# Emission order kept on every engine, a multiply-and-accumulate for the denominators, and first-tile silus in groups of two

## The chip, the cores and the metric

The kernel runs on one core of one Trainium2 chip. The metric is the device time of one execution in microseconds. Three timed runs of the kernel before gave 1099.16 us as the median, from 1097.7 to 1101.51. Names of engines are those of the profile: PE is the matmul engine, PEld its loads of weights, DVE the vector engine, ACT the activation engine, POOL the general engine, SP the engine that issues most DMAs. A line number such as L505 is a line of the kernel before; the kernel after is shorter by two to three lines there, and rows of its order carry its own numbers.

## The reference

Attention with random features over 8 batches of 8 heads, 576 tokens and 64 dimensions, followed by one layer of a perceptron with silu over the 4608 tokens. All of it is float32; the weights of the perceptron come as 64-bit floats.

```python
def phi(x):
    proj = np.einsum('bhsd,md->bhsm', x, omega)
    sq = np.sum(x * x, axis=-1, keepdims=True) / 2.0
    h = proj - sq
    h = h - np.max(h, axis=-1, keepdims=True)
    return np.exp(h) / np.sqrt(m)
q_p, k_p = (phi(q_s), phi(k_s))
kv = np.einsum('bhsm,bhsd->bhmd', k_p, v)
z = np.sum(k_p, axis=2)
num = np.einsum('bhsm,bhmd->bhsd', q_p, kv)
den = np.einsum('bhsm,bhm->bhs', q_p, z)[..., None] + 1e-06
attn = num / den
...
h = x @ w_in
g = h * (1.0 / (1.0 + np.exp(-h)))
out = g @ w_out
```

## The kernel before

**Attention.** It goes by pairs of heads, 32 of them (n = 0 to 31), each a `hk` and a `hq` of nine chunks of 128 tokens by 128 features. The middle chunk holds the last 64 tokens of one head and the first 64 of the other. For a pair, SP loads the raw keys and queries, the same in natural order (`nat`), and the values. ACT squares `nat` (L250) and DVE sums it (`sqk`, `sqq`, L254). PE projects (L262, and the middle chunk at L269), DVE takes the maxima (`mxk`, `mxq`, L276 and L278) and makes the shift `nbk`, `nbq` in two instructions (L282, L283). ACT does the exp: for the first eight pairs chunk by chunk from PSUM (L298), for the others DVE first lowers the values into SBUF (L303, L306) and one exp follows (L312). POOL adds the keys' chunks up to `es` (L318, L320, L323), PE sums `es` over the tokens and spreads the sum to all partitions (L327), ACT copies it to `zb` (L335, L336), three versions of 128 columns: one head, middle, other head. PE makes the product of keys and values (L343), ACT copies it (`kt`, L348), PE turns it (L351), ACT copies it again (`kw`, L356).

**Denominators.** DVE multiplies `hq` by `zb` in three instructions (chunks 0 to 3, 4, 5 to 8; L362) into `prod`, which has a 129th column of guard values in each chunk, set once by POOL (L219). DVE then sums `prod` over 129 columns into `den`, nine values per partition (L369), and takes the reciprocal `rd` (L370). POOL multiplies `hq` by `rd` in three groups of chunks (L375), PE transposes them (L381), ACT copies them to `en` (L385), and PE makes the numerator (L399), which is the attention's result: ACT writes its high part `xh` (L413), DVE the rest `xl` (L418).

**Weights.** There are 32 chunks of 512 KB, sixteen of each matrix. Each is loaded by SP (`wraw`, L435), and turned from 64-bit floats to 32-bit ones by ACT (`wre`, L442) and three DVE instructions (L456, L458, L462), then split by POOL into a high and a low part (L476, L480). The parts of the second matrix go out to HBM (L483) and are loaded again for each step (L487).

**Perceptron.** Nine tiles of 512 tokens: four pairs fill a tile, and the ninth holds the 64 tokens left over from each batch. A tile has 16 steps f of 128 hidden features, 144 steps in all. A step is stage one (L495, twelve matmuls into a bank `ps_h`), silu on ACT twice (`gh`, rounded, L500; and in place in PSUM, L501), `gl` on DVE, which is their difference and frees the bank (L505), and stage two (L513, twelve matmuls into four banks `ps_acc`).

**What sets the order.** The class `Plan` lists units of work with an engine, a duration, a key (when it is due) and what they need, simulates them, and picks for each engine the ready unit with the least key; a change of ACT's function adds 8 to the key and 1.3 to the duration. PSUM has two banks `h`, two `att` and four `acc`; attention may borrow from `h` and `acc` early on, by the key of the unit. The units are emitted in the order that `plan.run()` returns. The layer below, the tile framework, then places the emitted instructions on each engine, and moves instructions past one another as it sees fit where data allow it. Loads of tables for ACT's functions are added by the compiler where exp and silu alternate.

Of the kernel before, what the change touches and what calls it, by code (L numbers as in the profile page):

```python
# [8 lines left out]
F32 = mybir.dt.float32  # L9
# [4 lines left out]
ALU = mybir.AluOpType  # L14
# [4 lines left out]
P = 128  # L19
# [44 lines left out]
class Plan:  # L64
# [16 lines left out]
    def run(self):  # L81
# [29 lines left out]
        def bank_pools(u):  # L111
            pools = ["att"]
            if u["key"] < clock(LAG) - 1:
                pools.append("acc")
            if u["key"] < START_MLP - 1:
                pools.append("h")
            chosen, when, used = [], 0.0, {p: 0 for p in pools}
            for _ in range(u["banks"]):
                best = None
                for p in pools:  # L120
                    t = slot_time(p, used[p])
                    if t is not None and (best is None or t < best[0]):
                        best = (t, p)
                if best is None:
                    return None, None
                used[best[1]] += 1
                chosen.append(best[1])
                when = max(when, best[0])
            return chosen, when
# [68 lines left out]
def attention_mlp(ctx: ExitStack, tc: tile.TileContext, qT, kT, qn, kn, v, om_in, w_in, w_out, out):  # L198
# [16 lines left out]
    nc.vector.memset(ones, 1.0)  # L215
    omr = const.tile([P, M], F32, tag="omr", name="omr")
    oms = const.tile([P, M], F32, tag="oms", name="oms")
    prod = const.tile([P, NC, M + 1], F32, tag="prod", name="prod")
    nc.gpsimd.memset(prod, GUARD)  # L219

    def bank(pool):
        return pools[pool].tile([P, 512], F32, tag=pool, name=f"ps_{pool}")
# [132 lines left out]
        T["kw", n] = kw = new("kw", [P, P])  # L355
        nc.scalar.copy(kw, T.pop(("kwp", n))[:, :P])  # L356

    def products(n):
        e, zb = T["h", n, "q"], T.pop(("zb", n))
        for j, (lo, hi) in enumerate(((0, 4), (4, 5), (5, 9))):  # L360
            c = slice(lo, hi)
            nc.vector.tensor_tensor(  # L362
                prod[:, c, :M], e[:, c], zb[:, j].unsqueeze(1).broadcast_to([P, hi - lo, M]), ALU.mult
            )

    def denom(n):
        den = new("den", [P, NC])
        T["rd", n] = rd = new("rd", [P, NC])
        nc.vector.tensor_reduce(den, prod, AX.X, ALU.add)  # L369
        nc.vector.reciprocal(rd, den)  # L370

    def normal(n, g):
# [175 lines left out]
    for n in range(NWIN):  # L548
# [67 lines left out]
        if not merged:  # L616
# [5 lines left out]
            free=[("kt", n)])  # L622
        add(("kw", n), "ACT", 0.3, at(n, 6.8, 36.7), lambda n=n: kw_copy(n), after=[("ktt", n)], order=[("kw", n - 1)] if n else [],
            alloc=[("kw", ("kw", n))], free=[bk(("ktt", n))])
        add(("prod", n), "DVE", 1.7, at(n, 8, 34.2), lambda n=n: products(n),
            after=e["q"] + [("zc", n)], order=[("den", n - 1)] if n else [], free=[("zb", n)])
        add(("den", n), "DVE", 1.6, at(n, 8.1, 34.4), lambda n=n: denom(n), after=[("prod", n)],
            alloc=[("den", ("den", n)), ("rd", ("rd", n))])
        plan.freed_by[("den", n)] = [("den", n)]
        for g in range(3):  # L630
            add(("norm", n, g), "POOL", 0.85, at(n, 9 + 0.1 * g, 37 + 0.1 * g), lambda n=n, g=g: normal(n, g),
# [57 lines left out]
    for i, (t, f) in enumerate(steps):  # L689
        key = clock(i)  # L690
        late = i >= total - LAG
        add(("get", t, f), "SP", 0.42, clock(i + LAG - AHEAD_OUT), lambda t=t, f=f: get_weight(t, f),
            after=[("keep", f)], order=[("get",) + divmod(i - 1, NF)] if i else [],
            alloc=[("wo", ("wo", t, f))], lat=2.1)
        for k in range(NK):
            x = [("restin", k)] if t == B else [("xl", NPAIR * t + k, 0)]
            w = [("wlo", "in", f)] if t == 0 else []
            add(("s1", t, f, k), "PE", 0.69, key + 0.945 * k, lambda t=t, f=f, k=k: stage1(t, f, k),
                after=x + w, order=[done] if done else [], alloc=[] if k else [("h", ("ph", t, f))],
                free=[("x", t, k)] if f == NF - 1 else [])  # L700
            done = ("s1", t, f, k)
        add(("silu", t, f), "ACT", 1.22, key + STEP * 0.55, lambda t=t, f=f: silu(t, f), after=[("s1", t, f, NK - 1)],
            alloc=[("gh", ("gh", t, f))], table="silu")
        add(("gl", t, f), "DVE", 0.7, key + STEP * 0.7, lambda t=t, f=f: g_low(t, f), after=[("silu", t, f)],
            alloc=[("gl", ("gl", t, f))], free=[("ph", t, f)])
        for j in range(4):
            k2 = clock(i + LAG + 0.5) + 0.945 * j
            if late:
                k2 = clock(total) + 4 + 4 * j + i - total
            alloc = [("acc", ("po", t, x)) for x in range(4)] if f == 0 and j == 0 else []  # L710
            w = [("get", t, f)]
            prior = [("s2",) + divmod(i - 1, NF) + (3 if not late else j,)] if i and (late or not j) else []
            if j:
                prior.append(("s2", t, f, j - 1))
            add(("s2", t, f, j), "PE", 0.69, k2, lambda t=t, f=f, j=j: stage2(t, f, j),
                after=[("gl", t, f)] + w, order=prior, alloc=alloc,
                free=[("gh", t, f), ("gl", t, f), ("wo", t, f)] if j == 3 else [])
            if f == NF - 1:
                add(("store", t, j), "ACT", 0.62, k2 + 0.2, lambda t=t, j=j: store(t, j), after=[("s2", t, f, j)],
                    free=[("po", t, j)])  # L720
    for u in plan.run():
        u["fn"](*[bank(p) for p in u["pools"]])


_OUT = ((B * S, DMODEL), "float32")
# [48 lines left out]
```

## Time and profile before

| what | value |
|---|---|
| runs, median (lowest, highest) | 1099.16 us (1097.7, 1101.51) |
| the profiled execution | 1101.4 us |
| its span | 1099.3 us, so 2.1 us outside |
| mean granted clock of PE | 0.976 |
| PE busy | 1053.1 us, 96% of the span |
| DVE, ACT, POOL busy | 566.4, 583.1, 255.5 us |
| table loads of ACT at L312, L500 | 48 and 56, 1283 ns each |

The page gives, by line, what an engine did and what it waited for. Busy shares over the whole span say little here: the start has little PE work and the rest is full of it, so the stages are read one by one. `gl` (L505) comes once in a step, and its starts are the milestones by which steps are counted in what follows: the first is at 100.00 us, the second at 107.70, the seventeenth, which ends the first tile's sixteen, at 225.10.

### The profile page before, as it was taken

Reading aid. Unit: us, or ns where it says so; the run is one execution under the profiler, and the core shown is the slowest. Engines: PE = TensorE matmul, PEld = TensorE weight load, DVE = VectorE, ACT = ScalarE, POOL = GpSimd, SP = SyncE. Lnnn points to the kernel's source line nnn. Section 1 sums busy time; section 2 is a strip of 40 time slices with the busy share of each in tenths; the row PEclk is TensorE's granted clock in tenths of the full one; section 3 lists DMA queues with packets and bytes.
Section 4 is the critical chain, followed back from the end, with each engine's and each line's share of the span. In section 5 each row is a group of like instructions: output and inputs, shape, how many; then the busy total and the mean of one; then the engine's idle time right before and its main releaser. Section 6 shows DMA issues by size and latency. Waiting matters only on the chain.

```text
span 1099.3 us, 16192 instructions
## 1 busy us (share of the span) xinstructions
PE 1053.1 (96%) x5900; PEld 834.5 (76%) x5900; DVE 566.4 (52%) x1109; ACT 583.1 (53%) x1085; POOL 255.5 (23%) x327
## 2 busy tenths in 40 slices
PE   5677998899999999999999999999999999999998
PEld 4455776687877778777778777787877788888886
DVE  6788897745555455545555455555554431111111
ACT  5557878565556555555556555655565442222211
POOL 3666665411111111111111111111111110000000
PEclk7688999999999999999999999999999999999999
DMA  7576787553335443444345433533343226223323
GB/s 282 198 221 234 265 290 252 182 167 125 124 126 178 139 133 119 136 165 138 122 139 178 140 127 130 173 131 126 123 154 104 80 80 213 96 96 122 109 96 96
DMA packets 66526, 167.84 MB, mean 153 GB/s; under 512 B 15632, under 2 KB 15760, under 8 KB 66448
## 3 DMA queue, kind: packets, MB, share of 16 engines
q1 hardware_dynamic: 65984, 166.23, 45.6%
q8 instruction: 47, 0.77, 0.3%
q10 hardware_dynamic: 464, 0.59, 0.1%
q14 instruction: 31, 0.25, 0.1%
HBM read 146.87 MB, written 19.92 MB: 152 GB/s over the span
## 4 chain that ended last, share of the span: by engine, by line
PE 86%; DVE 5%; DMA 3%; ACT 3%; POOL 1%; issue 1%; SPq 0%; ACTq 0%; DVEq 0%; POOLq 0%
PE ps_acc L513 35%; PE ps_h L495 34%; PE ps_att L262 5%; PE ps_att L343 3%; PE ps_att L381 3%; PE ps_att L399 2%; DMA wraw<-w_out 1%; DMA nat<-qn 1%; PE ps_att L327 1%; PE ps_att L269 1%; DVE w L458 1%; ACT hq L298 1%; DVE w L462 1%; POOL hq L375 1%; DVE den L369 1%
## 5 line engine op out<-in xcount | busy, mean ns | idle before, releaser
L513 PE MATMUL ps_acc<-wo,gh 128*128 128x512 f32 x1152 | 369.9, 402 | 0.0
L500 ACT ACTIVATE gh<-ps_h 128x512 fp32r<-128x512 f32 x144 | 86.2, 599 | 295.9 <-PE ps_h L495 295.3
L505 DVE TENSOR_TENSOR gl<-ps_h,gh 128x512 fp32r<-128x512 f32 x144 | 99.1, 688 | 275.8 <-ACT ps_h L501 275.8
L513 PEld LDWEIGHTS ps_acc<-wo,gh 128*128 128x128 f32 x1152 | 207.1, 189 | 43.7
L495 PE MATMUL ps_h<-xh,wh 128*128 128x512 f32 x576 | 235.0, 409 | 0.3 <-ACT xh L413 0.3
L495 PE MATMUL ps_h<-xh,wl 128*128 128x512 f32 x576 | 226.7, 394 | 0.0
L495 PE MATMUL ps_h<-xl,wh 128*128 128x512 f32 x576 | 225.9, 392 | 0.0
L513 PE MATMUL ps_acc<-wo,gl 128*128 128x512 f32 x576 | 225.8, 392 | 0.0
L375 POOL TENSOR_TENSOR hq<-hq,rd 128x384 f32<-128x384 f32 x96 | 81.7, 879 | 421.4 <-DVE rd L370 396.5
L495 PEld LDWEIGHTS ps_h<-xh,wh 128*128 128x128 f32 x576 | 108.1, 188 | 24.7 <-issue 0.8
L513 PEld LDWEIGHTS ps_acc<-wo,gl 128*128 128x128 f32 x576 | 108.1, 188 | 24.2 <-issue 0.8
L495 PEld LDWEIGHTS ps_h<-xh,wl 128*128 128x128 f32 x576 | 108.1, 188 | 24.1
L495 PEld LDWEIGHTS ps_h<-xl,wh 128*128 128x128 f32 x576 | 108.5, 188 | 22.3 <-DVE xl L418 0.4
L312 ACT ACT_TABLE_LOAD x48 | 61.6, 1283 | 69.2 <-DVE hq L303 53.3
L318 POOL TENSOR_TENSOR t<-hk 128x256 f32<-128x256 f32 x64 | 48.8, 780 | 183.2 <-ACT hk L312 170.1
L278 DVE TENSOR_REDUCE mxq<-ps_att 128x4 f32<-128x512 f32 x57 | 37.2, 687 | 99.7 <-PE ps_att L262 99.6
L501 ACT ACTIVATE ps_h<-ps_h 128x512 f32<-128x512 f32 x144 | 85.3, 593 | 0.0
L500 ACT ACT_TABLE_LOAD x56 | 71.8, 1283 | 22.0 <-PE ps_h L495 21.3
L362 DVE TENSOR_TENSOR prod<-hq,zb 128x512 f32<-128x512 f32 (+1 forms) x96 | 52.3, 595 | 49.6 <-ACT zb L336 47.7
L250 ACT ACTIVATE nat<-nat 128x576 f32<-128x576 f32 x64 | 44.6, 703 | 20.3 <-DMA nat<-kn 12.3
L381 PE MATMUL ps_att<-ident,hq 128*128 128x128 f32 x261 | 41.1, 284 | 7.9 <-POOL wp L476 2.4
L278 DVE TENSOR_REDUCE mxk<-ps_att 128x4 f32<-128x512 f32 x55 | 35.6, 686 | 18.7 <-PE ps_att L262 18.7
(121 smaller groups left out, 1232.0 us busy)
## 6 DMA issues: line engine op xcount, KB each, us to landing
wo<-wo_d SPq DMA_DIRECT2D x144, 512.0 KB, 3.3
rawk<-kT SPq DMA_DIRECT2D x32, 352.0 KB, 3.0
rawq<-qT SPq DMA_DIRECT2D x32, 352.0 KB, 3.8
v<-v SPq DMA_DIRECT2D x32, 320.0 KB, 2.9
nat<-kn SPq DMA_DIRECT2D x32, 288.0 KB, 3.3
nat<-qn SPq DMA_DIRECT2D x32, 288.0 KB, 3.2
wraw<-w_in SPq DMA_DIRECT2D x16, 512.0 KB, 4.6
wraw<-w_out SPq DMA_DIRECT2D x16, 512.0 KB, 4.3
```

What stands on the lines that cost most here:

```text
L262: nc.tensor.matmul(ps[:, i * M : (i + 1) * M], raw[r, o : o + P], oms[r], start=True, stop=True)
L278: nc.vector.tensor_reduce(m[:, 5 * j : 5 * j + 4], ps.rearrange("p (c m) -> p c m", m=M), AX.X, ALU.max)
L312: nc.scalar.activation(h, h, AF.Exp)
L318: nc.gpsimd.tensor_tensor(t[:, j], e[:, 5 * j : 5 * j + 2], e[:, 5 * j + 2 : 5 * j + 4], ALU.add)
L362: nc.vector.tensor_tensor(prod[:, c, :M], e[:, c], zb[:, j].unsqueeze(1).broadcast_to([P, hi - lo, M]), ALU.mult)
L375: nc.gpsimd.tensor_tensor(e[:, c], e[:, c], rd[:, c].unsqueeze(2).broadcast_to([P, 3, M]), ALU.mult)
L381: nc.tensor.transpose(ps[:, i * P : (i + 1) * P], T["h", n, "q"][:, 3 * g + i], ident)
L495: nc.tensor.matmul(ph, w[:, k, :], x, start=k == 0 and n == 0, stop=k == NK - 1 and n == 2)
L500: nc.scalar.activation(gh, ph, AF.Silu)
L501: nc.scalar.activation(ph, ph, AF.Silu)
L505: nc.vector.tensor_tensor(gl, T["ph", t, f], T["gh", t, f].bitcast(F32), ALU.subtract)
L513: nc.tensor.matmul(T["po", t][j], g[:, js], w, start=f == 0 and n == 0, stop=f == NF - 1 and n == 2)
```

## The change

There are four edits.

1. The loop that emits the units stands in `tc.manual_schedule()`: the framework keeps the emitted order on every engine.
2. The three products and the sum of a pair's denominators become nine `tensor_tensor_reduce`, one per chunk, each multiplying `hq` by `zb`, adding up over the 128 columns from the start value GUARD, and giving one column of `den`. On DVE each is two instructions, the second of which reads the accumulator. `prod` loses its guard column and the memset on POOL. In the plan one unit `den` of 2.3 us takes the place of `prod` (1.7) and `den` (1.6).
3. In the first tile (t = 0) the silu of an even step waits for stage one of the odd step behind it, and its key is later by one step, so that two silus stand together.
4. Attention may no longer borrow banks `h` once the first stage one is placed.

```diff
-            if u["key"] < START_MLP - 1:
+            if u["key"] < START_MLP - 1 and ("s1", 0, 0, 0) not in end:
                 pools.append("h")
...
-    prod = const.tile([P, NC, M + 1], F32, tag="prod", name="prod")
-    nc.gpsimd.memset(prod, GUARD)
+    prod = const.tile([P, NC, M], F32, tag="prod", name="prod")
...
-    def products(n):
+    def denom(n):
         e, zb = T["h", n, "q"], T.pop(("zb", n))
-        for j, (lo, hi) in enumerate(((0, 4), (4, 5), (5, 9))):
-            c = slice(lo, hi)
-            nc.vector.tensor_tensor(
-                prod[:, c, :M], e[:, c], zb[:, j].unsqueeze(1).broadcast_to([P, hi - lo, M]), ALU.mult
+        den = new("den", [P, NC])
+        for c in range(NC):
+            j = (c >= MID) + (c > MID)
+            nc.vector.tensor_tensor_reduce(
+                out=prod[:, c], in0=e[:, c], in1=zb[:, j], scale=1.0, scalar=GUARD, op0=ALU.mult, op1=ALU.add,
+                accum_out=den[:, c : c + 1],
             )
-
-    def denom(n):
-        den = new("den", [P, NC])
         T["rd", n] = rd = new("rd", [P, NC])
-        nc.vector.tensor_reduce(den, prod, AX.X, ALU.add)
         nc.vector.reciprocal(rd, den)
...
-        add(("prod", n), "DVE", 1.7, at(n, 8, 34.2), lambda n=n: products(n),
-            after=e["q"] + [("zc", n)], order=[("den", n - 1)] if n else [], free=[("zb", n)])
-        add(("den", n), "DVE", 1.6, at(n, 8.1, 34.4), lambda n=n: denom(n), after=[("prod", n)],
-            alloc=[("den", ("den", n)), ("rd", ("rd", n))])
+        add(("den", n), "DVE", 2.3, at(n, 8, 34.2), lambda n=n: denom(n), after=e["q"] + [("zc", n)],
+            order=[("den", n - 1)] if n else [], alloc=[("den", ("den", n)), ("rd", ("rd", n))], free=[("zb", n)])
...
-        add(("silu", t, f), "ACT", 1.22, key + STEP * 0.55, lambda t=t, f=f: silu(t, f), after=[("s1", t, f, NK - 1)],
+        pair = t == 0 and f % 2 == 0
+        add(("silu", t, f), "ACT", 1.22, key + STEP * (1.55 if pair else 0.55), lambda t=t, f=f: silu(t, f),
+            after=[("s1", t, f + pair, NK - 1)],
             alloc=[("gh", ("gh", t, f))], table="silu")
...
-    for u in plan.run():
-        u["fn"](*[bank(p) for p in u["pools"]])
+    with tc.manual_schedule():
+        for u in plan.run():
+            u["fn"](*[bank(p) for p in u["pools"]])
```

How instructions stand on the engines, at three places. PE in the startup, between the transposes of pair 0 (`ident,hq`) and the projections of pair 2 (`oms,rawk`); `es,ones` is the sum over tokens of pair 1, `hk,v` its product of keys and values, `en,kw` the numerator of pair 0. Before:

```order
L381 MATMUL ps_att<-ident,hq 128x128 x6
L327 MATMUL ps_h<-es,ones 128x256
L343 MATMUL ps_att<-hk,v 64x128 x10
L399 MATMUL ps_acc<-en,kw 64x512 x2
L399 MATMUL ps_att<-en,kw 64x64 x2
L262 MATMUL ps_acc<-oms,rawk 128x128 x8
```

After:

```order
L378 MATMUL ps_att<-ident,hq 128x128 x6
L342 MATMUL ps_att<-hk,v 64x128 x10
L396 MATMUL ps_acc<-en,kw 64x512 x2
L396 MATMUL ps_att<-en,kw 64x64 x2
L326 MATMUL ps_acc<-es,ones 128x256
L350 MATMUL ps_acc<-ident,kt 128x128
```

The sum over tokens stood ahead of the other two and now stands behind them.

DVE at the denominators of pair 2; `sqq` is the sum of squares for the queries of pair 3, `mxk` maxima of the keys of later pairs. Before:

```order
L362 TENSOR_TENSOR prod<-hq,zb 128x4x128
L362 TENSOR_TENSOR prod<-hq,zb 128x128
L362 TENSOR_TENSOR prod<-hq,zb 128x4x128
L254 TENSOR_REDUCE sqq<-nat 128x9
L369 TENSOR_REDUCE den<-prod 128x9
L278 TENSOR_REDUCE mxk<-ps_att 128x4
L370 RECIPROCAL rd<-den 128x9
```

After, from the last of the nine chunks on:

```order
L362 ISA prod,den<-hq,zb 128x128
L362 ISA den 128x1
L367 RECIPROCAL rd<-den 128x9
L253 TENSOR_REDUCE sqq<-nat 128x9
L277 TENSOR_REDUCE mxk<-ps_att 128x4 x2
```

The sum of squares stood between the products and their sum, and now stands behind the reciprocal; nothing stands between the chunks.

ACT in the first tile, at the exps of the keys of pair 7 and the silus around them. Before:

```order
L298 ACTIVATE hk<-ps_att,nbk 128x128 x8
L385 COPY en<-ps_att 128x384
L500 ACT_TABLE_LOAD
L500 ACTIVATE gh<-ps_h 128x512
L385 COPY en<-ps_att 128x384
L298 ACT_TABLE_LOAD
L298 ACTIVATE hk<-ps_att,nbk 128x128
L501 ACT_TABLE_LOAD
L501 ACTIVATE ps_h<-ps_h 128x512
```

After:

```order
L297 ACTIVATE hk<-ps_att,nbk 128x128 x8
L382 COPY en<-ps_att 128x384
L497 ACT_TABLE_LOAD
L497 ACTIVATE gh<-ps_h 128x512
L498 ACTIVATE ps_h<-ps_h 128x512
L497 ACTIVATE gh<-ps_h 128x512
L498 ACTIVATE ps_h<-ps_h 128x512
L382 COPY en<-ps_att 128x384
L297 ACT_TABLE_LOAD
L297 ACTIVATE hk<-ps_att,nbk 128x128
```

One step's two activations stood on both sides of an exp with a table load ahead of each; now the four activations of two steps stand behind one load. Over the whole program the order has 120 table loads before and 108 after; up to the seventeenth `gh` there are 28 and 16.

## The prediction

> **What bounds the kernel now.** I read the table of stages first, then single starts of `gl`, then the chain of waits up to 225 us, then the timelines of DVE and ACT. The profiled execution took 1101.4 us, of which the span is 1099.3; 2.1 us lie outside it. The columns of the table are the stretch, its length, each engine's busy time with its count of instructions, TensorE's granted clock and the DMA share.
>
> ```profile
> core 0: us, PE busy (x) PEld busy (x) DVE busy (x) ACT busy (x) POOL busy (x), PEclk, DMA share, GB/s
> 0.00:107.70 107.70, 74.47 (x459) 52.77 (x460) 83.18 (x152) 66.83 (x191) 63.80 (x76) 0.76 0.70 233
> 107.70:225.10 117.40, 109.13 (x599) 82.97 (x598) 94.95 (x161) 89.22 (x169) 65.95 (x67) 1.00 0.71 242
> 250.00:850.00 600.00, 599.79 (x3546) 478.76 (x3545) 325.03 (x678) 340.02 (x572) 113.94 (x166) 1.00 0.42 138
> ```
>
> From 250 us on PE is never idle and runs at the full clock: every other engine has room, and only fewer matmuls could shorten that stretch. The change removes none. The idle PE time lies ahead: 33.2 us of it (107.7 − 74.47) before the second `gl`, at 107.70, and 8.3 us (117.4 − 109.13) in the first tile, up to the 17th, at 225.10. The next rows are the second and the seventeenth `gl`, and `gl` alone counted in the two last stretches.
>
> ```profile
> 107.70 0.69 DVE L505 TENSOR_TENSOR gl<-ps_h,gh 128x512 fp32r<-128x512 f32 x1
> 225.10 0.69 DVE L505 TENSOR_TENSOR gl<-ps_h,gh 128x512 fp32r<-128x512 f32 x1 [3.21 <-ACT ps_h L501]
> 107.70:225.10 117.40, 10.14 (x15) 1.00 0.71 242
> 250.00:850.00 600.00, 56.52 (x82) 1.00 0.42 138
> ```
>
> Fifteen steps take 117.4 us in the first tile, 7.83 each; later 82 take 600 us, 7.32 each. At the later pace the fifteen are 109.8 us. So the first tile has 7.6 us to give by its steps and 8.3 by PE's idle time, which agree. Everything behind 225.10, 874 us of the span, I take as unchanged: the order on PE there is the same in both kernels, and PE is full.
>
> In the startup DVE has 83.18 busy of 107.70 us, more than any other engine. Two places of it show what the order costs. On PE, for pair 1:
>
> ```profile
> 27.25 0.90 PE L381 MATMUL ps_att<-ident,hq 128*128 128x128 f32 x3 [0.33 <-POOL hq L375]
> 33.65 1.22 PE L327 MATMUL ps_h<-es,ones 128*128 128x256 f32 x2 [5.50 <-POOL es L323]
> 36.99 1.84 PE L399 MATMUL ps_acc<-en,kw 128*64 128x512 f32 x4
> ```
>
> PE stands 5.50 us for POOL's `es` of pair 1, with the k-v product of pair 1 and the numerator of pair 0 queued behind; pair 0's transposes ended at 28.15. And on DVE, for pairs 1 and 2:
>
> ```profile
> 40.87 0.88 DVE L362 TENSOR_TENSOR prod<-hq,zb 128x128 f32<-128x128 f32 x2
> 42.33 1.35 DVE L369 TENSOR_REDUCE den<-prod 128x9 f32<-128x1161 f32 x1
> 44.20 0.21 DVE L370 RECIPROCAL rd<-den 128x9 f32<-128x9 f32 x1
> 55.83 1.59 DVE L362 TENSOR_TENSOR prod<-hq,zb 128x512 f32<-128x512 f32 x3
> 58.83 0.76 DVE L254 TENSOR_REDUCE sqq<-nat 128x9 f32<-128x576 f32 x1 [1.41 <-ACT nat L250]
> 59.50 1.35 DVE L369 TENSOR_REDUCE den<-prod 128x9 f32<-128x1161 f32 x1
> 61.37 0.20 DVE L370 RECIPROCAL rd<-den 128x9 f32<-128x9 f32 x1
> ```
>
> Pair 2's products end at 57.42, yet `den` starts at 59.50, since a sum of squares whose square came late stands between. The chain shows what it waited for, and two durations:
>
> ```profile
> 19.25 1.49 DVE prod L362 x3
> 53.83 4.20 DMA nat<-qn
> 59.58 1.27 DVE den L369
> ```
>
> **The change, part by part. Order kept.** It moves rows on all five engines and adds no work. For pair 1 the k-v product and the numerator go ahead of the wait for `es`. They may start at about 28.5 rather than at 34.8 and 36.99. DVE then has the low part of pair 0 done before pair 1's `zb` (its sum ends at 34.87, four copies of ACT follow, about 36). The denominators of pair 1 may start near 36.2; with 2.4 us for them (below) and 0.12 for the reciprocal, `rd` is ready near 39 where it was at 44.20: 5 us. For pair 2 `den` no longer stands behind the late sum of squares: that is another 3 us at 61.37 (from 57.42, and 2.4 us of work that starts at 55.83, against 61.37), but the next pair's shift needs that same sum, and the load of `qn` (4.20 us) that it waits for isn't shortened, so I count pair 2's as partly hidden. What is late next is DVE's own work: 83.18 of 107.70 us. Bounds for the startup: 0, if other waits (the loads of `qn`, POOL's norms) take the place; 10, if both gains and some of the 24.5 idle DVE us go. I take 5, the gain of pair 1 alone, handed on whole.
>
> Against it, an order that is fixed can put DVE, ACT or SP behind a head that waits. Where a dependent pair stands together on DVE it costs little: the rows below show 0.20 from the start of the first to the start of the second (228.58 to 228.78) and 0.07 where a stranger follows (76.86 to 76.93), so 0.13 each. There are 20 more such pairs of shifts in the whole program and 32 of `den` and reciprocal; nine of 32 pairs of heads lie before 225.10, so at most (20 + 9) × 0.13, about 4 us of DVE, which the 24.5 idle us cover in part. I leave it in the lower half of the range.
>
> ```profile
> 228.58 0.17 DVE L282 TENSOR_TENSOR nbk<-mxk,sqk 128x8 f32<-128x8 f32 x1
> 228.78 0.17 DVE L283 SCALAR_TENSOR_TENSOR nbk<-nbk,sqk 128x8 f32<-128x8 f32 x1
> 97.29 0.28 DVE L276 TENSOR_REDUCE mxk<-ps_att 128x1 f32<-128x128 f32 x1
> 97.49 0.20 DVE L370 RECIPROCAL rd<-den 128x9 f32<-128x9 f32 x1
> 76.86 0.14 DVE L282 TENSOR_TENSOR nbk<-mxk,sqk 128x1 f32<-128x1 f32 x1
> 76.93 0.68 DVE L462 SCALAR_TENSOR_TENSOR w<-wraw,w 128x512 uint32<-128x512 uint32 x1
> 77.53 0.15 DVE L283 SCALAR_TENSOR_TENSOR nbk<-nbk,sqk 128x1 f32<-128x1 f32 x1
> ```
>
> **One multiply-and-accumulate per chunk.** Three products and one reduction, 1.49 + 1.27 = 2.76 us, become nine pairs of instructions: a 128x128 multiply with accumulation, and a read of the accumulator that writes 128x1. The trace has neither. The nearest rows: a 128-element operation takes 0.20 from its start to the next one's (97.29 to 97.49), a one-element operation 0.07 (76.86 to 76.93). Together 0.27, nine times 2.43: 0.33 us less than before for each pair of heads, 3 us of DVE for the nine up to 225.10. That is the low bound. At the high bound nothing overlaps: the whole durations, 0.28 + 0.14 = 0.42, nine times 3.78, 1.0 us more per pair. In the first tile the old form was dearer, as POOL works beside it:
>
> ```profile
> L362 DVE TENSOR_TENSOR prod<-hq,zb 128x512 f32<-128x512 f32 (+1 forms) x12 | 9.9, 853 | 3.4 <-ACT hq L312 1.9 <-ACT zb L336 1.5
> L369 DVE TENSOR_REDUCE den<-prod 128x9 f32<-128x1161 f32 x4 | 5.4, 1358 | 0.1
> ```
>
> (9.9 + 5.4) / 4 is 3.83 per pair, 1.39 times 2.76. If both prices stretch alike, the high bound is 9 × 0.42 × 1.39 = 5.25 there, 1.4 more per pair. Over five pairs of startup and four of the first tile the bounds are −3 and +10.8 us of DVE. I take the low value, since the rows by which consecutive DVE instructions start before the one ahead has ended are everywhere, and book it at 0: DVE has idle time in both stretches, and the 3 us lie within the 5 of the startup.
>
> [...]
>
> **Silus in groups of two.** In the first tile exp and silu alternate on ACT, and each change loads a table. Columns below: busy time, mean ns; the first rows are one silu of before, torn by an exp between its two activations.
>
> ```profile
> 186.50 1.28 ACT L500 ACT_TABLE_LOAD   x1
> 188.41 1.28 ACT L298 ACT_TABLE_LOAD   x1
> 190.35 1.28 ACT L501 ACT_TABLE_LOAD   x1
> 191.65 0.58 ACT L501 ACTIVATE ps_h<-ps_h 128x512 f32<-128x512 f32 x1
> L298 ACT ACT_TABLE_LOAD x10 | 12.8, 1283 | 5.0 <-DVE nbk L283 4.0 <-DVE nbq L283 0.9
> L500 ACT ACT_TABLE_LOAD x8 | 10.3, 1283 | 0.1
> L501 ACT ACT_TABLE_LOAD x4 | 5.1, 1283 | 0.1
> ```
>
> 22 loads there cost 28.2 us of ACT's 89.22. The whole program has 120 loads before and 108 now; the twelve, 15.4 us, all fall into the first tile. ACT then has 43 us to spare there, and the chain of waits, which runs through these loads between 146 and 157 us, loses them. The price is on PE. With two banks for `ps_h`, stage one of step f+2 needs `gl` of step f. Before, that was made while stage one of f+1 ran; now the silu of f waits for f+1, and one table load, two activations and `gl` (1.28 + 0.60 + 0.58 + 0.69 = 3.15, with hand-offs some 3.5 us) lie bare unless PE has something else. What it has is stage two of earlier steps and attention:
>
> ```profile
> 118.36 1.24 PE ps_att L343 x20
> 119.61 0.97 PE ps_att L399 x8
> 120.58 2.96 PE ps_acc L513 x12
> ```
>
> By the order 3.3 to 4.9 us of such work stand at five of the eight places, and only about 2 at the first. I sum 1.5 for the first and 0 to 0.4 for each of seven: 3 us. If the cover is late it is up to 3.5 eight times, 28 us. The bank that attention loses once stage one has begun, and the guard memset of POOL that goes (before any `prod`), I book at nothing: PE's first stage-one work is rare while attention still has six other banks, and POOL's first sum waits for ACT's exps anyway.
>
> **The sum.** Startup −5. First tile: the 8.3 us of idle PE less the 3 us of new stalls, −5.3. Together −10.3: 1101.4 − 10.3 = 1091.1 for a profiled execution. The median of the runs, 1099.16, lies 2.2 below the profiled one, so the prediction is **1089 us**.
>
> **The rivals.** (a) Both stretches give all that they hold: 10 in the startup, 8.3 in the first tile, none lost to pairs. 1101.4 − 18.3 − 2.2 = 1081. For it: DVE and ACT both lose work, and the chain there passes table loads; against it: DVE is at 77% in the startup and the loads of weights (DMA share 0.71) are not shortened. (b) The multiply-and-accumulate is dear, by +10.8 us of DVE: if all of it lands on the path, 1101.4 − 10.3 + 10.8 − 2.2 = 1099.7; if half, 1094. For it: DVE is the busiest engine of the startup; against it the rows with overlap. [...] (c) The order kept does nothing for the whole: pair 1's gain is swallowed by the next `qn` load, and the pairs' stalls eat the first tile's 8.3: 1099. (d) Slower: the pairs of silus stall PE. Place: stage one of every even step of the first tile, waiting for `gl` of the step two back. If only the k-v product (1.24) stands there, (3.5 − 1.24) × 8 = 18.1 us, against the 13.3 us of the rest: 1101.4 − 13.3 + 18.1 − 2.2 = 1104. It decides as soon as a stall is over 13.3 / 8 = 1.7 us, that is, as soon as less than 1.8 us of PE work covers each. For it: stage two of the step before needs weights that come by DMA and POOL and may be late; against it: the 2.96 us of stage two in the row above.
>
> **Chances and range.** Forecast 0.47, with its own range 1083 to 1094; (a) 0.15; (b) 0.15, a third of it the halved throughput; (c) 0.09; (d) 0.14. The range for 8 in 10 leaves out the ends of (a) and most of (d): 1077 to 1103. A measurement of this kernel can tell about 0.3%, 3.3 us, from no change. Faster than 1095.9: 0.47 + 0.15, a third of (b) and a little of (c), 0.68. Within: the rest of (b) and most of (c), 0.17. Slower than 1102.5: (d) and a bit, 0.15.
>
> **What would show it.** Right: the second `gl` near 103 rather than 107.7, fifteen steps after it in about 112 us, PE's wait for `es` at pair 1 gone or moved behind the numerator, `rd` of pair 1 near 39, about 14 table loads rather than 22 between the two `gl`, and the nine pairs of instructions in 2.4 to 2.6 us where POOL is idle. Wrong: nine pairs that take 3.7 us or more (b); waits of PE for `gl` of 1.7 us or more in the first tile, at more than two of the eight places (d); an unchanged time of the second `gl` (c); or any change of more than 1 us behind the seventeenth, which I hold to be fixed by PE.

## The result, and the profile after

The changed kernel takes 1093.29 us (median of five runs, 1092.94 to 1093.95) against 1099.23 for the kernel before (five runs, 1097.7 to 1101.51). The ratio is 0.9947, with a 95% interval from 0.9935 to 0.9959: faster by 5.9 us, where 10.2 were forecast and 1077 to 1103 was the range. The profiled execution took 1093.79 us, its span 1092.0. The spans of the two profiled executions, from which the parts below are read, differ by 7.3 us. The sign and the range held. Cut at the second `gl`, as the prediction does, the parts did not: the startup gave nearly twice what was forecast, and the first tile gave nothing. That cut isn't like for like, as is shown below. One of the nine runs of the groups alone took 1731.93 us at a mean granted clock of 0.554; its ratio is worked out without it, and the median of the other eight is 1103.2.

The table of stages of the changed kernel, cut at its second and seventeenth `gl`, with columns as before:

```profile
core 0: us, PE busy (x) PEld busy (x) DVE busy (x) ACT busy (x) POOL busy (x), PEclk, DMA share, GB/s
0.00:98.94 98.94, 65.01 (x447) 47.47 (x448) 87.03 (x226) 65.02 (x195) 59.25 (x75) 0.78 0.75 256
98.94:217.25 118.31, 111.49 (x614) 86.36 (x613) 90.82 (x213) 75.11 (x153) 64.33 (x64) 0.96 0.69 238
```

The startup is 98.94 us long where it was 107.70: 8.8 less. The fifteen steps of the first tile take 118.31 where they took 117.40: 0.9 more, at a mean clock of 0.96 rather than 1.00. Behind the seventeenth `gl` lie 1092.0 − 217.25 = 874.75 us of the span; before, 1099.3 − 225.10 = 874.20.

The groups make the first two `gl` come together, so the second one now marks an earlier point of the work. Before, 41 matmuls of the perceptron are on record ahead of it, 36 of stage one and 5 of stage two; now there are 25. A mark with the same work ahead of it is the last matmul of the third step's stage one. Its start in both kernels, and the stretch up to it, with 457 matmuls on record each:

```profile
107.24 0.40 PE L495 MATMUL ps_h<-xh,wl 128*128 128x512 f32 x1
102.90 0.40 PE L492 MATMUL ps_h<-xh,wl 128*128 128x512 f32 x1
0.00:107.24 107.24, 74.01 (x457) 52.40 (x458) 82.75 (x151) 66.81 (x190) 63.48 (x76) 0.76 0.69 232
0.00:102.90 102.90, 68.97 (x457) 50.53 (x458) 89.70 (x245) 68.92 (x203) 59.25 (x75) 0.77 0.74 254
```

Up to this mark the change gains 4.3 us, from there to the seventeenth `gl` 3.5 (117.86 to 114.35), and behind that it loses 0.55.

In the first tile PE's waits have nearly one cause now. The columns are the sum, the count and the longest; the first three rows are the largest waits of before, the last two are all of after:

```profile
PE ps_att L381 <- POOL wp L476: 2.4, 1, 2.4
PE ps_att L351 <- DVE xl L418: 2.0, 1, 2.0
PE ps_att L381 <- DVE hk L306: 1.4, 1, 1.4
PE ps_h L492 <- DVE gl L502: 9.0, 5, 3.2
PE ps_att L378 <- DVE hk L305: 1.0, 1, 1.0
```

The longest wait for `gl`, 3.2 us, ends at 98.68, just ahead of the second `gl`; the other four, 5.8 us, lie in the fifteen steps.

ACT's table loads there are 14, as the order said. Before there were 24: the 22 of the prediction leave out two at L312. The first row is of before:

```profile
L312 ACT ACT_TABLE_LOAD x2 | 2.6, 1283 | 0.8 <-DVE hq L303 0.6 <-DVE hk L303 0.2
L497 ACT ACT_TABLE_LOAD x7 | 9.0, 1283 | 0.1
L297 ACT ACT_TABLE_LOAD x6 | 7.7, 1283 | 3.5 <-DVE nbk L282 3.4
L311 ACT ACT_TABLE_LOAD x1 | 1.3, 1283 | 0.0
```

For pair 1, PE runs the product of keys and values and the numerator at once, and hardly waits for `es`:

```profile
24.36 2.40 PE L342 MATMUL ps_att<-hk,v 128*64 128x128 f32 x20
26.55 1.45 PE L396 MATMUL ps_acc<-en,kw 128*64 128x512 f32 x4
28.54 0.70 PE L326 MATMUL ps_acc<-es,ones 128*128 128x256 f32 x2 [0.43 <-POOL es L322]
```

And the new instructions for pair 0, the first two chunks and the reciprocal, on the timeline of DVE:

```profile
16.38 0.28 DVE L362 CUSTOM_DVE_ANT_0 prod<-hq,zb 128x128 f32<-128x128 f32 x1
16.59 0.08 DVE L362 DVE_READ_ACCUMULATOR2_ANT den<- 128x1 f32 x1
16.59 0.28 DVE L362 CUSTOM_DVE_ANT_0 prod<-hq,zb 128x128 f32<-128x128 f32 x1
...
18.41 0.21 DVE L367 RECIPROCAL rd<-den 128x9 f32<-128x9 f32 x1
```

Each chunk takes 0.21 us from start to start; the read of the accumulator starts together with the next multiply and adds next to nothing to the 0.20 that a 128-element operation took in the profile before (97.29 to 97.49). Nine take 2.03 us (16.38 to 18.41).

### The profile page after: what moved, and what is told of

Same layout as the page of the kernel before. It is cut to its first block, busy times and chain, and to the rows that moved or that the text cites. A ratio compares the mean times of both kernels' runs of the same rounds, so it can differ in the third digit from the quotient of the medians.

```text
span 1092.0 us, 16620 instructions
## 1 busy us (share of the span) xinstructions
PE 1043.7 (96%) x5900; PEld 829.4 (76%) x5900; DVE 539.8 (49%) x1557; ACT 568.3 (52%) x1073; POOL 251.8 (23%) x326
## 4 chain that ended last, share of the span: by engine, by line
PE 84%; DVE 7%; ACT 5%; issue 2%; DMA 2%; POOL 1%; ACTq 0%; SPq 0%; DVEq 0%; POOLq 0%
PE ps_h L492 35%; PE ps_acc L510 34%; PE ps_att L261 5%; PE ps_att L342 3%; PE ps_att L396 2%; PE ps_att L378 2%; PE ps_att L268 1%; PE ps_att L326 1%; DVE prod L362 1%; DMA nat<-qn 1%; ACT L497 1%; DMA out<-ot 1%; ACT hk L297 1%; DVE w L455 1%; DVE w L453 1%
## 5 line engine op out<-in xcount | busy, mean ns | idle before, releaser
L492 PE MATMUL ps_h<-xh,wh 128*128 128x512 f32 x576 | 238.2, 414 | 9.1 <-DVE gl L502 9.0
L362 DVE CUSTOM_DVE_ANT_0 prod<-hq,zb 128x128 f32<-128x128 f32 x288 | 67.2, 299 | 43.9 <-ACT zb L335 43.9
```

The lines of the kernel that those rows point to most:

```text
L362: nc.vector.tensor_tensor_reduce(out=prod[:, c], in0=e[:, c], in1=zb[:, j], scale=1.0, scalar=GUARD, op0=ALU.mult, op1=ALU.add, accum_out= ...
L492: nc.tensor.matmul(ph, w[:, k, :], x, start=k == 0 and n == 0, stop=k == NK - 1 and n == 2)
```

## The experiments

Twelve kernels ran, each beside the kernel before, whose median was between 1098.7 and 1100.0 in each set. The sets ran on different chips, so a difference across sets is also given against the kernel before beside each. The table has eleven of the kernels; the twelfth, with added matmuls, has a section of its own. "Groups" below always means the silus in groups of two with the rule on banks that goes with them: without that rule the plan finds no order at all once the silus are grouped, since attention then holds the bank that the second step needs.

| order kept | denominators | groups | plan's unit | us (median) | ratio to before, 95% |
|---|---|---|---|---|---|
| no | old | no | 1.7 + 1.6 | 1099.2 | 1 |
| yes | old | no | 1.7 + 1.6 | 1089.5 | 0.9903 [0.9878, 0.9928] |
| yes | new | no | 1.7 + 1.6 | 1084.7 | 0.9866 [0.9848, 0.9884] |
| yes | new | no | 3.3 | 1082.2 | 0.9836 [0.9821, 0.9851] |
| yes | new | no | 2.3 | 1094.0 | 0.9957 [0.9942, 0.9972] |
| yes | new | bank rule only | 2.3 | 1091.4 | 0.9928 [0.9901, 0.9955] |
| yes | old | yes | 1.7 + 1.6 | 1104.0 | 1.0032 [1.0019, 1.0045] |
| yes | new | yes | 1.7 + 1.6 | 1098.8 | 0.9997 [0.9987, 1.0007] |
| yes | old | yes | 2.3 | 1100.8 | 1.0020 [1.0009, 1.0030] |
| **yes** | **new** | **yes** | **2.3** | **1093.3** | **0.9947 [0.9935, 0.9959]** |
| no | new | no | 2.3 | 1103.8 | 1.0041 [1.0026, 1.0056] |
| no | old | yes | 1.7 + 1.6 | 1103.3 | 1.0042 [1.0027, 1.0056] |

The bold row is the change as it is; run once more beside the 1084.7 kernel it gave 1092.8 (0.9947 [0.9928, 0.9965]).

### The order alone

```diff
-    for u in plan.run():
-        u["fn"](*[bank(p) for p in u["pools"]])
+    with tc.manual_schedule():
+        for u in plan.run():
+            u["fn"](*[bank(p) for p in u["pools"]])
```

> Order kept, nothing else: the old products and sum, single silus. Theory (the order is worth about half of the startup's 9 us, the multiply-and-accumulate the rest): the second gl 4 to 5 us earlier than before, the first tile about as long as before (117 us for fifteen steps), total 1094 to 1096. Rival (the order does nothing by itself; DVE's shorter work is all): 1098 to 1100, with the reciprocal of pair 1 at 43 us or later.

Measured: 1089.54 us, 0.9903 [0.9878, 0.9928]. Its table of stages, cut at the second and seventeenth `gl`:

```profile
0.00:97.74 97.74, 67.24 (x451) 48.53 (x452) 89.00 (x149) 66.25 (x189) 59.09 (x72) 0.77 0.74 246
97.74:212.70 114.96, 107.36 (x608) 82.51 (x607) 101.51 (x165) 79.66 (x163) 69.09 (x72) 0.99 0.75 255
```

Both expectations were too high. The order by itself takes 10.0 us off the startup (9.0 by the last matmul of the third stage one) and 2.4 off the first tile (114.96 for 117.40), more than the whole change. So what came with it must, on balance, have cost.

### The order and the new denominators, without the groups

```diff
-        pair = t == 0 and f % 2 == 0
+        pair = False
```

> The changed kernel with single silus, so order kept, multiply-and-accumulate, no groups of two. Theory (the groups cost: PE waits 9.0 us for gl in the first tile and runs three times at a clock of 0.63 for it, 1.9 us each): 1093.3 less 5 to 9, so 1084 to 1088, PE's wait for gl near nothing and the fifteen steps in 110 to 113 us, though ACT has 8 more table loads. Rival (the groups pay for themselves by fewer table loads): 1093 to 1096.

Measured: 1091.39 us, 0.9928 [0.9901, 0.9955], between the two ranges. PE's wait for `gl` fell from 9.0 to 1.5 us, as expected, but the total fell by 1.9 only, the intervals overlap with the change's, and the fifteen steps took 121.2. Other waits had come in the place: 2.3 us for `es`, 2.0 for `hk`, 2.3 for `en`. So either the groups cost little, or this kernel has a fault of its own. The later runs speak for the second.

### The groups with the old denominators; the new denominators alone

The first of the two takes edit 2 back, instructions and units of the plan; the second is edit 2 alone on the kernel before, the same lines the other way round.

```diff
-        add(("den", n), "DVE", 2.3, at(n, 8, 34.2), lambda n=n: denom(n), after=e["q"] + [("zc", n)],
...
+        add(("prod", n), "DVE", 1.7, at(n, 8, 34.2), lambda n=n: products(n),
...
+        add(("den", n), "DVE", 1.6, at(n, 8.1, 34.4), lambda n=n: denom(n), after=[("prod", n)],
```

> The changed kernel with the old three products and one sum, so order kept and silus in groups of two. Theory (nine pairs of heads at 0.73 us each are 6.6 us of DVE ahead of the seventeenth gl, and DVE is busy 87 of 98.9 us in the startup): 4 to 6 us slower than the changed kernel, 1097 to 1099. Rival (DVE's work is covered by its idle time): 1093 to 1095.

Measured: 1104.03 us, 1.0032 [1.0019, 1.0045], worse than any theory. Beside the order alone, the groups with their rule on banks cost 14.5 us here. PE waits 9.8 us for `gl` in the first tile.

> The kernel before with the multiply-and-accumulate alone: the order is again set by the framework, silus single. Theory: 2 to 4 us faster than before, 1095 to 1097, less than the 6.6 us of DVE that it saves, since the head of PE still waits for es of pair 1. Rival (it is the whole gain): 1091 to 1094. Rival (without the kept order the rows are put so that it gains nothing): 1098 to 1100.

Measured: 1103.79 us, 1.0041 [1.0026, 1.0056], slower than before, which none of the three expected. PE waits here for weights, not for denominators:

```profile
PE ps_h L492 <- POOL wh L473: 5.2, 3, 2.4
PE ps_att L378 <- POOL wp L473: 3.0, 1, 3.0
```

The theory's reason failed too: PE's sum of `es` for pair 1 starts at 30.27, after a wait of 0.75 us, though the order was left to the framework. The reciprocals came early (pair 4 at 89.9 us, where it was 97.5), but the splits of the weights came late. In this run and in the one before, the plan also differs, since its units have other durations. Two runs therefore change the instructions and leave every row where it was.

### The price of the instruction, at a fixed order

The changed kernel, with products and sum written at the place of the nine:

```diff
-        for c in range(NC):
-            j = (c >= MID) + (c > MID)
-            nc.vector.tensor_tensor_reduce(
...
+        for j, (lo, hi) in enumerate(((0, 4), (4, 5), (5, 9))):
+            c = slice(lo, hi)
+            nc.vector.tensor_tensor(
+                prod[:, c, :M], e[:, c], zb[:, j].unsqueeze(1).broadcast_to([P, hi - lo, M]), ALU.mult
+            )
+        nc.vector.tensor_reduce(den, prod, AX.X, ALU.add)
```

> The changed kernel with its order as it is, row for row, but each nine multiply-and-accumulates written as the old three products and one sum at the same place. Theory (the instruction's price decides: nine pairs of heads at 0.7 us each, about 6 us of DVE ahead of the seventeenth gl): 1097 to 1100. Rival (the price is covered; the run with the old products was slow because its plan is another one): 1092 to 1095.

Measured: 1100.77 us, 1.0020 [1.0009, 1.0030], so 7.5 us more than the change (7.6 against the kernel before beside each), and a little above the theory's range. DVE's groups for the denominators in its startup (five pairs) and first tile (four), and then those of the changed kernel, both in the same order of stages:

```profile
L363 DVE TENSOR_TENSOR prod<-hq,zb 128x512 f32<-128x512 f32 x10 | 9.3, 928 | 0.0
L366 DVE TENSOR_REDUCE den<-prod 128x9 f32<-128x1161 f32 x5 | 6.8, 1365 | 0.2
L363 DVE TENSOR_TENSOR prod<-hq,zb 128x128 f32<-128x128 f32 x5 | 1.9, 389 | 0.0
...
L363 DVE TENSOR_TENSOR prod<-hq,zb 128x512 f32<-128x512 f32 (+1 forms) x12 | 6.0, 552 | 3.5 <-ACT zb L336 3.5
L366 DVE TENSOR_REDUCE den<-prod 128x9 f32<-128x1161 f32 x4 | 5.5, 1364 | 0.1
```

```profile
0.00:98.94 98.94, 13.49 (x90) 0.78 0.75 256
98.94:217.25 118.31, 7.98 (x72) 0.96 0.69 238
```

Old: (9.3 + 6.8 + 1.9) / 5 = 3.6 us per pair in the startup and (6.0 + 5.5) / 4 = 2.9 in the first tile. New: 13.49 / 5 = 2.7 and 7.98 / 4 = 2.0. That is 0.9 per pair, 8 us for nine, and the end comes 7.5 us later.

> The kernel with order kept and groups of two that ran 1104, its order as it is, row for row, but with multiply-and-accumulates in place of products and sum. Theory (price): 5 to 7 us faster than 1104, 1097 to 1099. Rival (order): 1101 to 1105.

Measured: 1098.83 us, 0.9997 [0.9987, 1.0007], 5.2 less than the 1104.0 of the same order with the old instructions (4.3 against the kernel before beside each). At both orders the price reaches the end, in the larger part at least.

### The same without groups

The order-alone kernel, with the nine in the place of products and sum, no row moved:

```diff
     def products(n):
         e, zb = T["h", n, "q"], T.pop(("zb", n))
+        T["den", n] = den = new("den", [P, NC])
+        for c in range(NC):
+            j = (c >= MID) + (c > MID)
+            nc.vector.tensor_tensor_reduce(
...
     def denom(n):
-        nc.vector.tensor_reduce(den, prod, AX.X, ALU.add)
-        nc.vector.reciprocal(rd, den)
+        nc.vector.reciprocal(rd, T.pop(("den", n)))
```

> The kernel with order kept alone (1089.5), its order as it is, row for row, but with multiply-and-accumulates in place of products and sum. Theory (the price, 0.7 us of DVE per pair of heads, is worth the same 5 to 7 us without the groups as with them): 1083 to 1086. Rival (the price counts only where the groups push DVE's work together; with single silus DVE's idle time covers it): 1088 to 1091.

Measured: 1084.73 us, 0.9866 [0.9848, 0.9884]: 4.8 less than with the old instructions (3.5 against the kernel before beside each, and the intervals of the two ratios just overlap), and 8 less than the changed kernel beside it. Its stages:

```profile
0.00:96.80 96.80, 64.38 (x457) 47.29 (x458) 85.85 (x219) 67.22 (x191) 55.83 (x71) 0.82 0.74 248
96.80:209.00 112.20, 104.66 (x602) 80.27 (x601) 97.59 (x221) 78.21 (x161) 69.24 (x72) 1.00 0.77 260
```

The first tile takes 112.2 us at the full clock. That is the number that was forecast for the change, and it comes without the groups.

### The groups in the framework's order

```diff
-            if u["key"] < START_MLP - 1:
+            if u["key"] < START_MLP - 1 and ("s1", 0, 0, 0) not in end:
...
-        add(("silu", t, f), "ACT", 1.22, key + STEP * 0.55, lambda t=t, f=f: silu(t, f), after=[("s1", t, f, NK - 1)],
+        pair = t == 0 and f % 2 == 0
+        add(("silu", t, f), "ACT", 1.22, key + STEP * (1.55 if pair else 0.55), lambda t=t, f=f: silu(t, f),
+            after=[("s1", t, f + pair, NK - 1)],
```

> The kernel before with the silus in groups of two and the rule on banks that they need, the old products and sum, and the order left to the framework. Theory (the groups cost in any order: PE waits for gl with nothing to do): 1103 to 1110, PE waiting 5 us or more for gl in the first tile. Rival (the framework puts other work into the gap): 1097 to 1101.

Measured: 1103.28 us, 1.0042 [1.0027, 1.0056], in the theory's range, but PE waits only 2.3 us for `gl`, and 7.0 us for the weights' parts from POOL. The theory's range was right and its reason wrong: the groups cost in this order too, but by another wait. That the framework put other work into the gap, as the rival said, fits this and isn't shown; the plan's rows differ as well.

### The stall and the clock

Where the wait for `gl` comes from, at step 6: stage one of step 5, for which the silu of step 4 waits, ends at 123.54, but ACT has exps of keys and a copy ahead of the table load.

```profile
123.15 0.39 PE L492 MATMUL ps_h<-xh,wl 128*128 128x512 f32 x1
123.01 2.18 ACT L297 ACTIVATE hk<-ps_att,nbk 128x128 f32<-128x128 f32 x8
125.26 0.48 ACT L382 COPY en<-ps_att 128x384 f32<-128x384 f32 x1
125.76 1.28 ACT L497 ACT_TABLE_LOAD   x1
127.06 0.60 ACT L497 ACTIVATE gh<-ps_h 128x512 fp32r<-128x512 f32 x1
```

In the changed kernel such a stall can cost twice. The window ahead of stage one of step 6, the twelve matmuls, and what follows; then the first of those matmuls, and the one at step 8:

```profile
125.20:129.00 3.80, 1.97 (x12) 1.38 (x11) 2.53 (x6) 3.71 (x6) 1.47 (x2) 1.00 0.92 329
129.00:133.60 4.60, 4.59 (x14) 3.58 (x15) 2.44 (x4) 3.33 (x6) 1.48 (x3) 0.63 0.53 184
133.60:138.90 5.30, 5.30 (x37) 4.24 (x35) 3.58 (x8) 1.71 (x5) 1.99 (x3) 1.00 0.31 100
```

```profile
129.01 0.47 PE L492 MATMUL ps_h<-xh,wh 128*128 128x512 f32 x1 [1.84 <-DVE gl L502]
145.21 0.50 PE L492 MATMUL ps_h<-xh,wh 128*128 128x512 f32 x1 [1.09 <-DVE gl L502]
```

After waits of 3.21, 1.84 and 1.82 us (at 98.68, 129.01 and 163.21) the granted clock is 0.63 over the next 4.6 us, and the twelve matmuls take 4.6 us from the start of the first to the end of the last. After waits of 1.09 and 1.03 us (at 145.21 and 179.42) it stays at 1.00, and they take 3.0. So each of the three costs 1.6 us more, where the expectations book 1.9. To test it, zeros were added to a bank of stage two ahead of the waits; every other row keeps its place:

```diff
+            if n[0] == "s1" and n[1] == 0 and n[2] in (4, 6, 8, 10, 12, 14) and n[3] == 0:
+                for _ in range(WARM):
+                    nc.tensor.matmul(T["po", 0][0][:, :P], zeros, ones, start=False, stop=False)
```

> The changed kernel, order kept row for row, with six 128x128 float32 matmuls with zeros (about 1.3 us, added to a bank of stage two, so they change no value) ahead of stage one of steps 4, 6, 8, 10, 12 and 14 of the first tile, where PE waits for gl. Theory (the clock falls to 0.63 for 3.5 us because PE stood still for 1.8 us, and costs 1.9 us each time): at steps 6 and 10 the clock stays at 1.00 and the total is 3 to 4 us less, 1089 to 1091; where PE waits 1.0 us only, 0.3 us is lost. Rival (the clock falls for another reason, or the wait alone counts): 1093 to 1095.

Measured: 1096.25 us, 0.9970 [0.9958, 0.9983], 3 us more than the change. The clock did what the theory said:

```profile
128.34 1.50 PE L725 MATMUL ps_acc<-ones,zeros 128*128 128x128 f32 x12
130.35 0.47 PE L494 MATMUL ps_h<-xh,wh 128*128 128x512 f32 x1 [0.51 <-DVE gl L504]
```

```profile
128.30:133.60 5.30, 4.79 (x29) 4.03 (x29) 2.97 (x6) 5.26 (x10) 0.83 (x2) 1.00 0.74 235
```

At step 6, the place shown, the clock stays at 1.00 from 128.30 to 133.60, where it was 0.63, so there it was standing still that lowered it. But the gain did not follow. The added matmuls also stand ahead of step 4, where PE had no wait, and put its stage one and all behind it 1.2 us later (115.00 rather than 113.76); stage one of step 6 starts at 130.35 rather than 129.01. The seventeenth `gl` came 0.5 us earlier only, at 216.7, and 3.5 us are lost behind it. In its profile PE stands 2.3 us in the fourth tile, and the chain goes back to a load:

```profile
457.62 5.44 DMA nat<-kn
...
476.76 0.67 PE L328 MATMUL ps_att<-es,ones 128*128 128x256 f32 x2 [2.25 <-DVE xl L417]
```

ACT's square waits for that load at the head of its queue, with exp, silu and `xh` behind it in a fixed order. The changed kernel has one wait of this kind too, 1.6 us at 824.82, behind a copy of ACT (`ot`) that stood for a store. That the filled kernel should have more of them is not explained; one profile cannot show whether it does in each run.

### Which row order: the bank rule and the plan's duration

```diff
-            if u["key"] < START_MLP - 1 and ("s1", 0, 0, 0) not in end:
+            if u["key"] < START_MLP - 1:
```

> Order kept and multiply-and-accumulate, silus single, and attention may borrow banks h as before (so the change without the groups and without the rule on banks). It ran 1091.4 with the rule on banks, and 1089.5 with the old products and no rule. Theory (DVE's saving of 6 us counts in the startup, and the rule on banks hides it): 1085 to 1088. Rival (DVE has idle time enough once the order is kept, so nothing): 1089 to 1092.

Measured: 1093.95 us, 0.9957 [0.9942, 0.9972], above both ranges. It has the same instructions as the 1084.7 kernel, with other rows first, because the plan has one unit of 2.3 us and not two of 1.7 + 1.6. Its second `gl` is at 91.1, the earliest of all, but then:

```profile
PE ps_h L492 <- POOL wh L473: 5.2, 2, 4.3
PE ps_att L378 <- ACT hk L297: 2.0, 1, 2.0
```

Attention ran ahead (the reciprocal of pair 4 starts at 79.87, where the 1084.7 kernel has 86.00) and the weights came late. The last run changes one number of the plan:

```diff
-        add(("den", n), "DVE", 2.3, at(n, 8, 34.2), lambda n=n: denom(n), after=e["q"] + [("zc", n)],
+        add(("den", n), "DVE", 3.3, at(n, 8, 34.2), lambda n=n: denom(n), after=e["q"] + [("zc", n)],
```

> Order kept and multiply-and-accumulate, single silus, no rule on banks: the kernel that ran 1094.0, but with the plan's unit for the denominators at 3.3 us, the sum of the two old units, in place of 2.3. Instructions and data are the same; only the order of rows moves. Theory (a unit that the plan believes shorter pulls attention ahead, and the weights' words and high parts come late, 5.2 us of PE waiting for them in that run): 1083 to 1087, PE's wait for POOL's wh gone. Rival (the merged unit or chance in the plan makes the difference, not the number): 1090 to 1095.

Measured: 1082.23 us, 0.9836 [0.9821, 0.9851], the best of all and just below the theory's range: 11.7 us less than with 2.3, for the same work. Its stages:

```profile
0.00:94.30 94.30, 66.04 (x450) 48.49 (x451) 84.97 (x218) 67.08 (x190) 55.65 (x70) 0.78 0.75 254
94.30:205.80 111.50, 106.92 (x609) 82.74 (x608) 98.92 (x222) 79.02 (x161) 70.27 (x73) 1.00 0.74 257
```

The wait for `wh` is gone. The units are merged here too, so the merging isn't what cost; that chance in the plan's rows did is not excluded. It beats the kernel before by 17.5 us and the changed one by 11. One more run repeated the change:

> The changed kernel as it is, on the chip of the run with order kept and multiply-and-accumulate. Theory and rival alike: 1092 to 1095, so that the two may be set side by side.

Measured: 1092.76 us, 0.9947 [0.9928, 0.9965].

## Why the prediction was right, and where it was not

**The sum.** Forecast −5 in the startup and −5.3 in the first tile; measured −8.8 and +0.9 by the second `gl`, and +0.55 behind the seventeenth: 1099.3 − 8.8 + 0.9 + 0.6 is the 1092.0 of the span. Cut where both kernels have done the same work, it is −4.3 and −3.5, near the forecast. That is in part luck, since the terms behind these sums were off both ways: the order and the new instructions gave more than was booked, the groups took more, and the time fell into the range as these partly cancelled. The prediction drew its gain from PE's idle time. Up to the seventeenth `gl` that is 41.50 us before and 40.75 after, of which 9.0 are the new waits for `gl`: the rest fell by 9.7, in the fifteen steps from 8.3 to 1.0. The other 7.1 us went from PE's busy time (183.60 to 176.50, for 1057 and 1060 matmuls on record), at a mean clock that is no higher (0.89 and 0.87); no term held this, and why it fell is open.

**The order.** The mechanism was right: `es` of pair 1 no longer stops PE (5.50 us before, 0.43 after), and the reciprocals come early, at 34.41 us for pair 1, where 39 was expected. The size was off. The prediction counted "the gain of pair 1 alone, handed on whole", 5 us. The order alone took 10.0 off the startup by the second `gl`, 9.0 by the last matmul of the third stage one, near the upper bound of 10 that it had set: the reciprocal of pair 0 was already 3.9 us early (19.4 in that run, 23.3 before), and pair 4's was 10.8 early.

**The multiply-and-accumulate.** The step that failed is "I take the low value ... and book it at 0: DVE has idle time in both stretches". At a fixed order it is worth 4.8 us without the groups, 5.2 and 7.5 with them (3.5, 4.3 and 7.6 against the kernel before beside each). Two numbers were wrong. The price is 0.21 per chunk while POOL is idle (16.38 to 18.41), not 0.27, as the accumulator's read adds next to nothing (one multiply beside POOL's `wp`, which runs from 31.23 to 32.51, took 1.13 us, at 31.54); and the old form costs 3.6 us per pair in the startup of the changed order, and 3.1 in the kernel before (7.2 + 6.8 + 1.4 over five pairs), not the 2.76 that was used there. And DVE's idle time does not cover it, as the three fixed orders show: 24.5 us of idle in a stretch says little when the work that ends it waits for DVE.

**The halved throughput**, to which the chances give a third of (b), is a term that no run of this case shows. What the changed kernel shows in its place: the multiply lasts 0.28 us for 128 elements (16.59), as the 128-element maximum does (97.29 in the profile before), with two float32 sources and the sum in it. Rival (b) falls, since the nine chunks of a pair take 2.03 us while POOL is idle (16.38 to 18.41) and not 3.7.

**The groups.** The step that failed is "I sum 1.5 for the first and 0 to 0.4 for each of seven: 3 us". The waits were 3.21, 1.84, 1.09, 1.82 and 1.03, together 9.0. At the three long ones work did stand ahead; it ran out before `gl` came, since `gl` waits for a table load that itself stands behind exps and copies on ACT. The prediction had put the chain at 3.5 us from the end of stage one and didn't add what ACT does first: at these three places it took 4.8, 5.5 and 5.6 us, with the load 1.7 to 2.5 us late. What it left out altogether is the clock: three of the five waits cost 1.6 us more (4.6 for the twelve matmuls, not 3.0). 9.0 + 4.8 is the order of the 14 us that the groups cost where all else is as like as it can be (1084.7 to 1098.8, 1089.5 to 1104.0). Up to the seventeenth `gl`, the first of these two differences is 7.5 us more of idle PE and 6.3 more of busy PE, for the same 1057 matmuls on record; the second is 12.3 and 0.9. The rows move with the groups, so this isn't the groups' waits alone. Rival (d) was this mechanism; its threshold of 1.7 us was passed at three places, more than the two that the prediction had named as its sign, and only the larger gains elsewhere kept the total on the fast side.

**The table loads** fell to 14 as counted, from 24 and not 22, and no gain from it shows: with instructions and units alike, the grouped kernel is slower by 14 us with the kept order (1104.0 to 1089.5, 1098.8 to 1084.7), by 4.6 with the framework's (1103.3 to 1098.7 beside it), and with the unit of 2.3 us about equal (1093.3 to 1091.4 and 1094.0). What PE waits for in the changed kernel is still ACT, by way of `gl`; fewer loads in all did not bring those silus earlier.

**The tail** was to stay within 1 us, and does (+0.55). But PE's idle time between 217 and 1080 us rose from 0.2 to 2.2 us, with two waits for `xl` of 1.55 and 0.40 us, so PE wasn't quite as full there as the prediction held.

**What no term held** is the plan's own duration. The change gave the new unit 2.3 us, near its real 2.0 to 2.7, in place of 3.3. That moves rows on all engines, and without the groups it costs 11.7 us (1094.0 to 1082.2). The prediction looked at the order in three places, all of them better than before, and not at where the weights' splits now stood. With the groups the same number does good (1098.8 to 1093.3, with the merged unit), so the effect belongs to a plan, not to the number. Why a longer duration gives the better rows was shown only as far as the wait for `wh` goes; the rest stays open.

## What to carry to other kernels

Where a planner's numbers set the order, time a change of instructions with every row held in place, and a change of rows with the instructions held: here each moves the time by as much as the whole edit, and the parts do not add. Before two short activations are put together to save a table load, ask what the matmul engine has to do until the second is done, and count what stands ahead of the load; a saved load is worth nothing if the activations behind the others come no earlier. Before two kernels are compared stage by stage, see that the mark between the stages has the same work ahead of it in both. Idle time of an engine over a stretch covers new work only if the stretch does not end in a wait for it.

## What the runs showed of the hardware

- Behind waits on PE of 1.84 and 1.82 us inside dense work, and behind one of 3.21 (129.01, 163.21 and 98.68 in the changed kernel), the clock was at half for about 3.4 us (matmuls 0.43 us apart rather than 0.23, from 129.79 to 133.18), beginning 0.3 to 0.9 us after the restart; behind waits of 1.09 and 1.03 us (145.21 and 179.42) it was not. Other waits left it at 1.00: 2.38 us at 169.49 in the kernel before (1.00 from 169.49 to 174.00), and 2.6 us in the first tile of the 1084.7 kernel (1.00 in each stretch of 10 us from 90 to 230). So the length alone doesn't decide. Matmuls with zeros in the gap ahead of step 6 kept the clock at 1.00 there (128.30 to 133.60).
- The read of the accumulator behind a multiply-and-accumulate starts with the next multiply (both at 16.59) and is all but free: 0.21 us per chunk of 128x128 with the read, 0.20 for a 128-element maximum without one (97.29 to 97.49 in the kernel before).
- A table load takes 1.28 us, and the activation behind it starts at once: in the chain of the changed kernel the copy ahead of a load ends at 95.52, the load starts at 95.53 and its silu at 96.82.
